# Turning the keys with 32x32 VectorE block transposes instead of TensorE transposes in a one-token decode block

## The chip, the cores and the metric

The kernel runs on one core of a Trainium2 chip. The metric is the time in device microseconds of one execution of the whole program. Five engines work side by side (in the kernel before, the three busiest are at work for 66%, 41% and 40% of the span): TensorE (PE in the profile; its weight loads are PEld), VectorE (DVE), ScalarE (ACT), GpSimd (POOL) and SyncE (SP), which here only issues transfers. In this kernel the data lie in on-chip tiles of 128 partitions; matmul results go to tiles that the kernel declares in a memory of their own, PSUM, in pieces that it calls banks (their names end in `_ps`).

TensorE runs at a granted clock, which the profile shows as a share of full speed (on average 0.803 in the profiled run of the kernel before).

## The reference, cut to what matters

One token, one layer: layer norm, attention over a cache of 65,536 keys and values, output projection, residual; then layer norm, a gated feed-forward of width 3,584, residual. There are 32 query heads and 4 key/value heads, so 8 query heads share one cache head.

```python
B, Sq, D = 1, 1, 1024
Hq, Hkv, Sk, Dh = 32, 4, 65536, 128          # k_cache, v_cache: (1, 4, 65536, 128) bf16
scores = einsum("bhqd,bhkd->bhqk", q, k) * Dh ** -0.5
p = softmax(scores); o = einsum("bhqk,bhkd->bhqd", p, v)
h  = x + o.reshape(1, 1, 4096) @ wo
h2 = h + (gelu(ln(h) @ w_gate) * (ln(h) @ w_up)) @ w_down   # F = 3584
```

The two caches hold 67 MB each; with the weights the kernel moves 173 MB, and every byte is used once. There is little arithmetic for each byte.

## The kernel before

All large inputs go through one queue and five rotating buffers of 4 MB (16,384 bf16 in each partition). A load is issued when the buffer that was filled five loads earlier is free again.

```python
NBUF = 5; CW = 16384
chpool = ctx.enter_context(tc.tile_pool(name="chpool", bufs=NBUF))
def load(src, name):
    t = chpool.tile([P, CW], BF16, name=name, tag="ch")
    ...
    nc.sync.dma_start(out=tv, in_=src)
```

Scores need the keys with the head dimension on the partitions, but they arrive with positions on the partitions. The kernel turns them on TensorE (two bf16 read as one f32, 128x128 at a time), and VectorE and ScalarE copy the result back out of PSUM:

```python
for c in range(NBK):
    kt_ps = ps_kt.tile([P, NB2, P], F32, name="kt_ps", tag="ktps")
    for b in range(NB2):
        nc.tensor.transpose(out=kt_ps[:, b, :], in_=k32s[...], identity=ident_f[:])   # L216
    if act_for(g, ci, c): nc.scalar.copy(out=dst_bf, in_=src_bf)                      # L220
    else:                 nc.vector.tensor_copy(out=dst_bf, in_=src_bf)               # L222
...
# scores: four column groups of 32, each matmul with its own weights
nc.tensor.matmul(qk_ps[32*c:32*c+32, :], lhsT=qsel[:, g, par, hf, :], rhs=..., tile_position=(0, 32*c))
...
nc.vector.transpose(out=sl..., in_=qk_ps[:])                                  # L245, 128x512
nc.vector.tensor_reduce(out=st["mx"][:, :, pi], in_=..., op=ALU.max)          # L246
```

When a head's scores are complete, the overall maximum is found, ScalarE takes the exponentials, and the values are multiplied while the keys of the next head arrive. So the first head is a stage of keys alone, the next three heads alternate keys and values, and the last head's values come alone. At the end comes the down projection, its weights in loads of 14, 7, 4, 2 and 1 rows of 128:

```python
def pair_mm(bank, stat, w2, c, first, last):     # the first 14 rows; 4 column groups, one bank
    for s in range(DS):
        g = 2 * s + c % 2
        nc.tensor.matmul(bank[32*g:32*g+32, :], lhsT=stat, rhs=w2[:, s*512:(s+1)*512], ..., tile_position=(0, 32*g))
# then cp_sum: 4 f32 matmuls against hsel add the column groups (hd_cp_ps);
# the last 14 rows: 8 matmuls each, 112 in all, one column out (dl_ps)
```

## Time and profile before

The median is 412.04 us over four runs (411.92 to 412.26). The profiled execution spans 410.2 us at a mean granted clock of 0.803.

| | before |
|---|---|
| moved by the main queue | 173.02 MB, 98.1% of 16 engines' span |
| rate between 20 and 390 us | 427 to 433 GB/s in each of seven stretches |
| TensorE / VectorE / ScalarE busy | 66% / 41% / 40% |
| first 14 rows of the down projection landed | 398.42 us |
| from there to the end | 11.8 us |

These are lines of the page of the kernel before: busy microseconds of each engine, two rows of the span cut into 40 slices (DMA in tenths of busy time, then GB/s), the engines' shares of the chain that ended last, and four groups of instructions (busy us, mean ns of one, then idle time before them and what ended it).

```profile
PE 271.7 (66%) x2577; PEld 193.1 (47%) x2577; DVE 168.9 (41%) x292; ACT 162.9 (40%) x249; POOL 5.1 (1%) x16
...
DMA  8999999999999999999999999999999999999993
GB/s 358 412 457 407 457 408 449 419 439 428 430 436 428 439 417 451 411 449 415 447 421 439 425 428 439 427 441 427 441 424 441 428 433 425 433 441 411 446 415 163
...
DMA 51%; PE 21%; ACT 6%; DVE 4%; issue 2%; DVEq 0%
...
L216 PE MATMUL kt_ps<-ident_f,k_sb 128*128 128x128 f32 x1024 | 144.5, 304 | 37.4 <-DMA k_sb<-in_A_k_cache_dram 34.4
L222 DVE COPY kt_sb<-kt_ps 128x1024 bf16<-128x1024 bf16 x140 | 95.3, 688 | 92.9 <-PE kt_ps L216 89.7
L246 DVE TENSOR_REDUCE mx<-sc_sb 128x8 f32<-128x512 f32 x32 | 35.2, 1100 | 0.5
L245 DVE STREAM_TRANSPOSE sc_sb<-qk_ps 128x512 f32<-128x512 f32 x32 | 23.0, 717 | 19.0 <-PE qk_ps L239 18.7
```

The DMA row never falls below nine tenths between the first and the last slice, and L216 waits almost only for keys to land. The transfers are the bottleneck; the engines run at their pace.

One 4 MB load (4.19 million bytes) takes 9.7 us at 431 GB/s.

Only the end of the program is not hidden behind transfers. This is the timeline of TensorE there (start, duration, engine, line, operation, count, and in brackets the idle time before it and what ended it):

```profile
398.42 2.66 PE L353 MATMUL d_ps<-wd_sb,actz 128*32 128x512 bf16 x28 [2.72 <-DMA wd_sb<-in_B_w_down_dram]
401.87 1.87 PE L382 MATMUL hd_cp_ps<-hsel,d_r 128*128 128x2 f32 x8 [0.79 <-DVE d_r L461]
403.60 2.50 PE L456 MATMUL dl_ps<-act_bf,wd_sb 128*128 128x1 bf16 x88
406.32 1.01 PE L456 MATMUL dl_ps<-act_bf,wd_sb 128*128 128x1 bf16 x24 [0.21 <-DMA wd_sb<-in_B_w_down_dram]
```

The last 24 matmuls wait a fifth of a microsecond for the last weights to land, so even this tail is balanced between TensorE and the queue.

### The profile page before, as it was taken

To read this page: it belongs to the slowest core of one execution; us is meant where nothing else is said; L and a number is where in the kernel's file an instruction comes from. 1 tells how busy PE (TensorE), PEld (TensorE's weight loads), DVE (VectorE), ACT (ScalarE), POOL (GpSimd) and SP (SyncE) were. 2 spreads that over 40 slices of the span, in tenths; PEclk is the share of its full clock that TensorE was granted. 3 is DMA by queue.
4 is the path that set the end of the run, shared out by engine and by line. 5 is a ranking of instruction groups with operands and counts; after the bars stand their busy time and mean duration, and the time that the engine had idled before them with its cause. 6 is when DMAs were issued, how large, how long until landed. Compare 5 with 4: busy or idle time off the path is not lost.

```text
span 410.2 us, 5998 instructions
## 1 busy us (share of the span) xinstructions
PE 271.7 (66%) x2577; PEld 193.1 (47%) x2577; DVE 168.9 (41%) x292; ACT 162.9 (40%) x249; POOL 5.1 (1%) x16
## 2 busy tenths in 40 slices
PE   0448888797994938964858399394945526467266
PEld 0227666484673727644555277182822213163135
DVE  0213787766772636751727086344630001022011
ACT  0014676597570648641525775152638000000000
POOL 1000000000000000000000000000020000000000
PEclk9986999969998886996969689979875655557665
DMA  8999999999999999999999999999999999999993
GB/s 358 412 457 407 457 408 449 419 439 428 430 436 428 439 417 451 411 449 415 447 421 439 425 428 439 427 441 427 441 424 441 428 433 425 433 441 411 446 415 163
DMA packets 6682, 173.40 MB, mean 423 GB/s; under 512 B 896, under 2 KB 896, under 8 KB 1152
## 3 DMA queue, kind: packets, MB, share of 16 engines
q1 hardware_dynamic: 6496, 173.02, 98.1%
q8 instruction: 20, 0.33, 0.3%
q14 instruction: 6, 0.05, 0.0%
q10 hardware_dynamic: 160, 0.00, 0.0%
HBM read 173.02 MB, written 0.00 MB: 422 GB/s over the span
## 4 chain that ended last, share of the span: by engine, by line
DMA 51%; PE 21%; ACT 6%; DVE 4%; issue 2%; DVEq 0%
DMA k_sb<-in_A_k_cache_dram 27%; PE kt_ps L216 13%; DMA wo_sb<-in_A_wo_dram 11%; DMA wu_sb<-in_B_w_up_dram 10%; ACT pT L272 4%; DMA wd_sb<-in_B_w_down_dram 3%; PE qk_ps L239 3%; ACT kt_sb L220 2%; PE acc_ps L289 2%; DVE mx L246 1%; PE at_ps L353 1%; PE wu_ps L158 1%; DVE kt_sb L222 1%; DVE sc_sb L245 1%; PE o_ps L305 1%
## 5 line engine op out<-in xcount | busy, mean ns | idle before, releaser
L216 PE MATMUL kt_ps<-ident_f,k_sb 128*128 128x128 f32 x1024 | 144.5, 304 | 37.4 <-DMA k_sb<-in_A_k_cache_dram 34.4
L216 PEld LDWEIGHTS kt_ps<-ident_f,k_sb 128*128 128x128 f32 x1024 | 131.6, 158 | 58.1 <-issue 36.6
L220 ACT COPY kt_sb<-kt_ps 128x1024 bf16<-128x1024 bf16 x116 | 111.9, 1016 | 105.5 <-issue 74.8
L222 DVE COPY kt_sb<-kt_ps 128x1024 bf16<-128x1024 bf16 x140 | 95.3, 688 | 92.9 <-PE kt_ps L216 89.7
L272 ACT ACTIVATE pT<-sc_sb,nbias 128x256 bf16<-128x256 f32 x64 | 47.5, 746 | 23.7 <-DVE nbias L264 23.7
L239 PE MATMUL qk_ps<-kt_sb,qsel 128*32 128x512 bf16 x512 | 39.6, 384 | 9.9 <-ACT kt_sb L220 9.2
L289 PE MATMUL acc_ps<-v_sb,pT 128*32 128x512 bf16 x512 | 37.4, 441 | 12.2 <-DMA v_sb<-in_A_v_cache_dram 12.2
L246 DVE TENSOR_REDUCE mx<-sc_sb 128x8 f32<-128x512 f32 x32 | 35.2, 1100 | 0.5
L245 DVE STREAM_TRANSPOSE sc_sb<-qk_ps 128x512 f32<-128x512 f32 x32 | 23.0, 717 | 19.0 <-PE qk_ps L239 18.7
L289 PEld LDWEIGHTS <-pT 128*32 128x32 bf16 x512 | 16.8, 107 | 28.9 <-issue 19.9
L165 ACT COPY wg_ev<-wg_ps 96x512 f32<-96x512 f32 x1 | 0.6, 582 | 59.4 <-PE wg_ps L158 59.4
L239 PEld LDWEIGHTS <-qsel 128*32 128x32 bf16 x512 | 8.3, 94 | 24.5 <-DVE kt_sb L222 15.2
L298 PE MATMUL l_ps<-lpart,ones_f 128*128 128x8 f32 x16 | 3.8, 312 | 21.7 <-ACT pT L272 21.7
L298 PEld LDWEIGHTS l_ps<-lpart,ones_f 128*128 128x128 f32 x16 | 3.2, 249 | 23.9 <-ACT pT L272 23.1
L158 PEld LDWEIGHTS <-hnz 128*32 128x32 bf16 x112 | 5.0, 127 | 17.6 <-issue 15.6
L158 PE MATMUL wu_ps<-wu_sb,hnz 128*32 128x512 bf16 x56 | 6.6, 579 | 9.3 <-DMA wu_sb<-in_B_w_up_dram 9.3
L353 PE MATMUL at_ps<-wo_sb,o2z 128*32 128x512 bf16 x64 | 7.2, 630 | 8.3 <-DMA wo_sb<-in_A_wo_dram 8.3
L272 ACT ACTIVATION_READ_ACCUMULATOR pT<-sc_sb,nbias 128x1 f32 x64 | 12.1, 190 | 0.0
L302 DVE COPY acc_sb<-acc_ps 128x512 f32<-128x512 f32 x4 | 2.7, 684 | 22.7 <-PE acc_ps L289 22.7
L165 ACT ACT_TABLE_LOAD x1 | 1.3, 1283 | 25.8 <-DVE q_ev L163 25.8
L125 PE MATMUL ln_tot<-ln_s,ones_f 128*128 128x1 f32 x4 | 1.2, 363 | 13.9 <-DVE ln_s L123 13.9
L353 PEld LDWEIGHTS <-o2z 128*32 128x32 bf16 x64 | 2.7, 140 | 12.0 <-issue 11.5
(108 smaller groups left out, 93.0 us busy)
## 6 DMA issues: line engine op xcount, KB each, us to landing
k_sb<-in_A_k_cache_dram SPq DMA_DIRECT2D x16, 4096.0 KB, 40.2
v_sb<-in_A_v_cache_dram SPq DMA_DIRECT2D x16, 4096.0 KB, 37.5
wq_sb<-in_A_wq_dram SPq DMA_DIRECT2D x2, 4096.0 KB, 16.8
wo_sb<-in_A_wo_dram SPq DMA_DIRECT2D x2, 4096.0 KB, 43.3
wg_sb<-in_B_w_gate_dram SPq DMA_DIRECT2D x2, 3584.0 KB, 43.7
wu_sb<-in_B_w_up_dram SPq DMA_DIRECT2D x2, 3584.0 KB, 40.6
wd_sb<-in_B_w_down_dram SPq DMA_DIRECT2D x1, 3584.0 KB
wd_sb<-in_B_w_down_dram SPq DMA_DIRECT2D x1, 1792.0 KB, 29.6
```

The costliest lines, as they stand in the source:

```text
L158: nc.tensor.matmul(banks[s // 4][32 * g:32 * g + 32, :], lhsT=stat, rhs=mov(s), start=first, stop=last, tile_position=(0, 32 * g))
L216: nc.tensor.transpose(out=kt_ps[:, b, :], in_=k32s[m0 // 16][:, m0 % 16, :], identity=ident_f[:])
L220: nc.scalar.copy(out=dst_bf, in_=src_bf)
L222: nc.vector.tensor_copy(out=dst_bf, in_=src_bf)
L239: nc.tensor.matmul(qk_ps[32 * c:32 * c + 32, :], lhsT=qsel[:, g, par, hf, :], rhs=mv[:, :, 32 * c:32 * c + 32, par], start=(hf == 0 and pa ...
L245: nc.vector.transpose(out=sl.rearrange("p n h -> p (n h)"), in_=qk_ps[:])
L246: nc.vector.tensor_reduce(out=st["mx"][:, :, pi], in_=sl.rearrange("p n h -> p h n"), axis=AX.X, op=ALU.max)
L272: nc.scalar.activation(out=pT[:, :, r, :], in_=sc_sb[:, hf * HG * TG:(hf + 1) * HG * TG, r].rearrange("p (a t) -> p a t", t=TG), func=ACT. ...
L289: nc.tensor.matmul(acc[32 * c:32 * c + rep * TG, :], lhsT=pTs[a // HG][:, a % HG, :, :].rearrange("p r t -> p (r t)"), rhs=v_sb[:, i * TG: ...
L298: nc.tensor.matmul(l_ps[:], lhsT=ones_f[:], rhs=lpart[:, hf, :], start=(hf == 0), stop=(hf == NH - 1))
L305: nc.tensor.matmul(o_ps[:], lhsT=acc_sb[:, t * Dh:(t + 1) * Dh], rhs=sel[:, t:rep * TG:TG], start=(t == 0), stop=(t == TG - 1))
L353: nc.tensor.matmul(bank[32 * g:32 * g + 32, :], lhsT=stat, rhs=w2[:, s * 512:(s + 1) * 512], start=first, stop=last, tile_position=(0, 32 ...
```

## The change

The intent is to take the transposes of the keys off TensorE and the copies off VectorE and ScalarE, and to load fewer weights.

1. VectorE turns the keys in place, 32x32 blocks of 32-bit words, four instructions of 128x2048 for each load. The copies of `kt_ps` go away.
2. A block-wise transpose leaves four positions' worth of data on the four quarters of the partitions. Query weights of 128x128 that hold the queries on the diagonal blocks and zeros elsewhere (`wsel`) take care of that: 32 matmuls of 512 columns for each load.
3. A weight load serves two matmuls in the scores, four in the values, and several in the projections. For this the order of TensorE is fixed by explicit dependencies.
4. The down projection puts both halves of a row in the same column group, and 21 of its 28 rows go this way instead of 14.

The diff, cut to its core (`mm` is a helper that emits a matmul, reuses the loaded weights where `loaded` is set, and chains it behind the one before; `evac` alternates VectorE and ScalarE):

```diff
-    ps_kt = ...(bufs=4, space=PSUM)   -    ps_qk = ...(bufs=2, space=PSUM)
+    ps_qk = actx.enter_context(tc.tile_pool(name="ps_qk", bufs=1, space=PSUM))
...
+    def k_load(g, li):
+        kt = kv_load(k_v[g], li, "k_sb").rearrange("p n d -> p (n d)").bitcast(U32)
+        for c in range(NSP):                                     # NSP = 4
+            nc.vector.transpose(out=kt[:, c * w:(c + 1) * w], in_=kt[:, c * w:(c + 1) * w])
...
+    def k_scores(g, li):
+        qk_ps = ps_qk.tile([P, 2, 512], F32, name="qk_ps", tag="qkps")
+        for a in range(TG):
+            for bp in range(4):
+                for k in range(2):
+                    mm(qk_ps[:, k, :], wsel[:, o:o + P], kt[:, a, k, :, bp // 2, :, bp % 2], ..., loaded=(k == 1))
+        nc.vector.transpose(out=sl..., in_=qk_ps[:]...)                      # 128x1024
+        nc.vector.tensor_reduce(out=st["mx"][:, :, li], ..., op=ALU.max)
+        if li == NL - 1:
             softmax_head(g)
...
-            acc_sb = ...; nc.vector.tensor_copy(out=acc_sb[:], in_=acc[:])
+            for c in range(4):
+                evac(acc_sb[32 * c:32 * c + 32, :], acc[32 * c:32 * c + 32, c, :], c)
...
+        for li in range(NL):
+            k_load(g, li)
+            if g >= 1: v_load(g - 1, li)
+            k_scores(g, li)
+            if g >= 1: v_values(g - 1, li)
...
-    def pair_mm(bank, stat, w2, c, first, last):
-            g = 2 * s + c % 2
+    def row_mm(banks, stat, w2, c, first, last):
+        g = c % 4
+        for s in range(DS):
+            mm(banks[s][32 * g:32 * g + 32, :], stat, w2[:, s * 512:(s + 1) * 512], first, last,
+               loaded=(s > 0), tile_position=(0, 32 * g))
...
-            nc.tensor.matmul(ps[:, b, :], lhsT=row[:, b * P:(b + 1) * P], rhs=hsel[:], ...)
+            for s in range(DS):
+                mm(ps[:, b, s:s + 1], row[:, s, b * P:(b + 1) * P], ones_f[:, 0:1], True, True)
...
-    NW = sizes[0]
+    NW = 21
```

## The prediction

> **What bounds it now.** The DMA. The page's DMA row stands at nine tenths or more in every slice but the first and last, queue 1 fills 98.1% of the 16 engines' span, and the windows view shows 429 to 435 GB/s from 5 us to about 380 us whatever the engines do. [...] 173.02 MB at 431 GB/s is 401.4 us of the 410.2 us span; about 2 us of start and 6 to 7 us of tail remain. The other engines (TensorE 66% busy) hide behind it. So only the tail, or a new starvation of the DMA queue, can move the time.
>
> **Removed.** 1024 f32 TensorE transposes (144.5 us busy), 256 copies of kt_ps (ScalarE 111.9, VectorE 95.3 us), about half of the weight loads.
>
> **Added.** 64 in-place VectorE transposes 128x2048. The 128x512 one takes 717 ns; [...] I estimate 2.3 us each, 9.2 us per K load. Score transpose and maximum now come as 1024 wide, estimated 1.25 and 2.2 us. With a wait for TensorE's last matmuls, VectorE needs about 15 us per K load. K and V scores become 1024 full-array matmuls of 512 columns, 0.21 us at full clock: 6.9 us per load of 9.7 us.
>
> **Consequence, main part.** With K and V alternating there are 19.4 us per K load: fits. In the first head K loads come every 9.7 us, so VectorE falls about 20 us behind; the five buffers nearly absorb it. My tightest point is the first V buffer's release, at about 113 to 119 us, against about 117 us when the queue needs it. Stall: 0 to 4 us in 95 to 130 us, more likely none.
>
> **Consequence, tail.** Down-projection rows: before, 28 matmuls ran four at a time (2.66 us from 398.4 us); now both matmuls of a row sit in one column group, so about two at a time: 15 slots of 0.21 to 0.43 us for 14 rows, and seven more rows (8 slots) after the 7-row load, all before the partial sums. Those sums have 16 passes for 8 (1.87 us before). Then 56 column matmuls for 112, but after all that. Estimate: TensorE ends 1.5 us (full clock) to 7 us (half clock) later than the 407.3 us of before; granted clock there was 0.5, so middle +3.5 us. This lies wholly on the critical path.
>
> **Prediction.** 415.5 us, 80% range 411 to 420.5. Faster by over 2%: 0.02; within 2%: 0.84; slower by over 2%: 0.14.
>
> **What would show it.** DMA row still nine tenths, about 431 GB/s. VectorE 55 to 60% busy, ScalarE under 20%, weight loading much lower. k_sb transposes 2.2 to 2.4 us. GB/s dips only between 95 and 130 us. In the chain of waits the end is TensorE's d_ps, hd_cp_ps, dl_ps work instead of the wd_sb landing; final dl_ps matmul at about 411 us.
>
> **What would make it wrong.** (a) The 32-bit SBUF transposes run at half rate: VectorE then needs over 20 us per K load, +30 us or more. (b) The clock stays at half during the V-only stage: 13.7 us per load exceeds 9.7, and the backlog reaches the tail. (c) The tail's clock is full, or TensorE runs the row matmuls more concurrently: then 411 to 412 us. (d) VectorE's doubled SBUF traffic slows the DMA.

The sum: 412.0 us of the kernel before + 0 us of stall + 3.5 us of tail = 415.5 us. The 15 us for each load of keys can also be estimated from the trace of the kernel before alone, in proportion to the elements: 16 × 717 ns for the keys, 2 × 717 ns for the scores and 2 × 1100 ns for the maximum are 15.1 us, without the wait.

## More of the kernel before

The next view is the table of stretches. Its columns are the stretch, its length, the busy time of PE, PEld, DVE, ACT and POOL with the number of instructions, the granted clock, the DMA share and GB/s.

```profile
60.00:100.00 40.00, 33.42 (x309) 24.93 (x308) 27.43 (x42) 29.17 (x50) 0.00 (x0) 0.91 1.00 432
100.00:130.00 30.00, 22.58 (x252) 16.28 (x250) 18.85 (x26) 15.32 (x16) 0.00 (x0) 0.99 1.00 431
180.00:200.00 20.00, 12.14 (x116) 9.86 (x109) 7.20 (x10) 6.05 (x7) 0.00 (x0) 0.83 0.99 427
```

The rate is nearly the same in all three, 427 to 432 GB/s, whatever the engines do.

## The result, and the profile after

The median is 414.97 us over four runs (414.42 to 415.13). The ratio to the kernel before is 1.0065, with a 95% interval of 1.0051 to 1.008. By the 2% measure the time is the same; by the interval it is a little longer.

The page of the kernel after, the lines that answer to those above:

```profile
PE 305.6 (74%) x1521; PEld 71.5 (17%) x732; DVE 216.0 (52%) x192; ACT 59.2 (14%) x151; POOL 12.3 (3%) x17
...
GB/s 356 409 454 419 443 419 444 420 441 422 397 408 451 416 447 418 441 416 400 447 416 452 409 454 409 451 411 451 412 451 411 447 416 447 419 430 428 426 414 151
...
DVE 42%; PE 34%; DMA 10%; ACT 9%; issue 5%; SPq 0%; ACTq 0%; DVEq 0%
...
L246 DVE STREAM_TRANSPOSE k_sb<-k_sb 128x2048 uint32<-128x2048 uint32 x64 | 143.0, 2279 | 0.1
L114 PE MATMUL qk_ps<-k_sb,wsel 128*128 128x512 bf16 x256 | 105.0, 410 | 23.5 <-DVE k_sb L246 23.0
...
L264 DVE STREAM_TRANSPOSE sc_sb<-qk_ps 128x1024 f32<-128x1024 f32 x16 | 20.0, 1248 | 46.0 <-PE qk_ps L116 33.9
L265 DVE TENSOR_REDUCE mx<-sc_sb 128x8 f32<-128x1024 f32 x16 | 31.8, 1987 | 0.4
```

The engines' work changed a great deal: ScalarE went from 40% to 14%, weight loading from 47% to 17%, VectorE from 41% to 52%. The chain that ended last was half DMA before; now it is mostly VectorE and TensorE. But the GB/s row is nearly as before, except in slices 11 and 12 (397 and 408, about 103 to 124 us) and slice 19 (400, about 186 to 196 us). The stretches show the same:

```profile
60.00:100.00 40.00, 20.48 (x72) 4.27 (x37) 36.30 (x22) 0.55 (x1) 0.00 (x0) 0.81 1.01 432
100.00:130.00 30.00, 28.15 (x117) 4.53 (x44) 16.53 (x10) 11.43 (x32) 0.00 (x0) 0.92 0.96 406
...
180.00:200.00 20.00, 19.94 (x85) 3.37 (x33) 14.59 (x9) 0.00 (x0) 0.00 (x0) 0.91 0.97 408
```

The queue ran partly dry twice: 406 GB/s instead of 431 for 30 us, and 408 instead of 427 for 20 us. By arithmetic that is 30 × (1 − 406/431) = 1.7 us and 20 × (1 − 408/427) = 0.9 us of lost transfer time. Take these as rough: stretches of 20 us scatter by about 10 GB/s where nothing runs dry (in this kernel 420 in 220 to 240 us, 441 in 240 to 260 us).

A split of the profiled span (410.2 to 413.1, so +2.9 us) at the landing of the first 14 rows of the down projection gives the size of both parts: the landing moved from 398.42 to 400.32 us (+1.9), and what follows it grew from 11.8 to 12.8 us (+1.0). So about two thirds came from dry spells of the queue and one third from the tail.

**The first dry spell.** This is the timeline of the kernel after, around the end of the first head:

```profile
95.79 0.15 DVE L273 TENSOR_REDUCE mx<-mx 128x8 f32<-128x32 f32 x1
95.85 2.30 DVE L246 STREAM_TRANSPOSE k_sb<-k_sb 128x2048 uint32<-128x2048 uint32 x1
...
98.07 0.24 DVE L277 TENSOR_REDUCE gm<-mxT_ps 8x1 f32<-8x128 f32 x1
...
99.14 0.61 PE L114 MATMUL qk_ps<-k_sb,wsel 128*128 128x512 bf16 x1
...
99.45 0.76 ACT L291 ACTIVATE pT<-sc_sb,nbias 128x256 bf16<-128x256 f32 x1 [61.39 <-DVE nbias L283]
...
108.75 0.38 PE L116 MATMUL qk_ps<-k_sb,wsel 128*128 128x512 bf16 x1
...
109.15 0.33 SPq L131 DMA_DIRECT2D v_sb<-in_A_v_cache_dram  x1
```

Read it from the bottom. The load issued at 109.15 us needs the buffer of the fifth load of keys (the second head's first). Its last score matmul starts at 108.75. The first started at 99.14, behind the first head's maximum, which VectorE finished late because it had been busy with keys nearly all the time (36.3 us of the 40 before 100 us). The rhythm of the first head shows why: the issues that wait for the first head's key buffers come 13.9 us apart (46.47, 60.40, 74.33 and 88.25 us), each after the last score matmuls of a load, which themselves wait for VectorE's last transpose of it, while keys arrive every 9.7 us. VectorE falls behind by about 4 us for each load, and five buffers do not quite cover it. In the kernel before, the corresponding load was issued at 95.68 us.

The fifth load's scores also ran slowly at first. After TensorE's wait the first 14 matmuls start 0.43 us apart, at a granted clock of 0.50 (99.1 to 105.06 us); only from 105.06 us, 5.9 us after the first of them, they start 0.216 us apart, at a clock of 1.00 (105.06 to 109.2 us). The third head's first scores do the same: 5.9 us at a clock of 0.51 from 177.73 us, then 1.00 from 183.60 us. In e3 below the same scores run slow for only 3.4 us (100.70 to 104.08), so the length varies; what sets it is not shown.

**The second dry spell.** The exponentials of a head stand on ScalarE ahead of two of the four copies of the previous head's values:

```profile
174.04 0.58 ACT L202 COPY acc_sb<-acc_ps 32x512 f32<-32x512 f32 x1
...
176.01 1.87 PE L114 MATMUL o_ps<-sel,acc_sb 128*128 128x8 f32 x8 [7.97 <-ACT acc_sb L202]
...
187.69 0.33 SPq L131 DMA_DIRECT2D v_sb<-in_A_v_cache_dram  x1
```

TensorE stood idle for 7.97 us before the matmuls that read these copies, started the third head's first scores only at 177.73 us, and the buffer they free went back to the queue at 187.69. ScalarE did its work here in the order in which it was given: VectorE's copy of the first quarter of the same values started at 167.95 us, but ScalarE took eight exponentials first (168.01 to 174.02 us) and only then its own copy, at 174.04.

**The tail.** The timeline of TensorE in the kernel after:

```profile
400.32 0.62 PE L114 MATMUL d_ps<-wd_sb,actz 128*32 128x512 bf16 x4 [3.35 <-DMA wd_sb<-in_B_w_down_dram]
400.70 0.67 PE L116 MATMUL d_ps<-wd_sb,actz 128*32 128x512 bf16 x4
...
406.82 1.95 PE L114 MATMUL hd_cp_ps<-ones_f,d_r 128*128 128x1 f32 x16 [0.79 <-DVE d_r L200]
408.62 1.62 PE L114 MATMUL dl_ps<-act_bf,wd_sb 128*128 128x1 bf16 x56
```

The partial sums start at 406.82 instead of 401.87 us, because they wait for the second load's rows too; with half as many column matmuls behind them, the end is only about a microsecond further from the first landing than before.

### The profile page after: what moved, and what is told of

Same layout as the page of the kernel before. It is cut to its first block, busy times and chain, and to the rows that moved or that the text cites. A ratio compares the mean times of both kernels' runs of the same rounds, so it can differ in the third digit from the quotient of the medians.

```text
span 413.1 us, 2802 instructions
## 1 busy us (share of the span) xinstructions
PE 305.6 (74%) x1521; PEld 71.5 (17%) x732; DVE 216.0 (52%) x192; ACT 59.2 (14%) x151; POOL 12.3 (3%) x17
## 4 chain that ended last, share of the span: by engine, by line
DVE 42%; PE 34%; DMA 10%; ACT 9%; issue 5%; SPq 0%; ACTq 0%; DVEq 0%
DVE k_sb L246 30%; PE acc_ps L116 10%; ACT pT L291 7%; PE qk_ps L114 5%; DMA wq_sb<-in_A_wq_dram 5%; PE qk_ps L116 5%; DVE sc_sb L264 5%; DMA wd_sb<-in_B_w_down_dram 4%; DVE mx L265 4%; PE acc_ps L114 4%; PE o_ps L114 2%; ACT acc_sb L202 1%; PE hc_ps L114 1%; DVE acc_sb L200 1%; PE h_cp_ps L114 1%
## 5 line engine op out<-in xcount | busy, mean ns | idle before, releaser
L246 DVE STREAM_TRANSPOSE k_sb<-k_sb 128x2048 uint32<-128x2048 uint32 x64 | 143.0, 2279 | 0.1
L114 PE MATMUL qk_ps<-k_sb,wsel 128*128 128x512 bf16 x256 | 105.0, 410 | 23.5 <-DVE k_sb L246 23.0
L116 PE MATMUL acc_ps<-v_sb,pT 128*128 128x512 bf16 x384 | 110.0, 397 | 0.0
L116 PE MATMUL qk_ps<-k_sb,wsel 128*128 128x512 bf16 x256 | 104.8, 409 | 0.0
L114 PE MATMUL acc_ps<-v_sb,pT 128*128 128x512 bf16 x128 | 51.0, 399 | 0.0
L114 PEld LDWEIGHTS <-wsel 128*128 128x128 bf16 x256 | 26.5, 104 | 128.5 <-issue 106.9
L264 DVE STREAM_TRANSPOSE sc_sb<-qk_ps 128x1024 f32<-128x1024 f32 x16 | 20.0, 1248 | 46.0 <-PE qk_ps L116 33.9
L265 DVE TENSOR_REDUCE mx<-sc_sb 128x8 f32<-128x1024 f32 x16 | 31.8, 1987 | 0.4
L114 PEld LDWEIGHTS <-pT 128*128 128x128 bf16 x128 | 13.2, 103 | 97.8 <-issue 97.7
L114 PE MATMUL o_ps<-sel,acc_sb 128*128 128x8 f32 x32 | 7.5, 364 | 26.6 <-ACT acc_sb L202 26.6
L114 PEld LDWEIGHTS o_ps<-sel,acc_sb 128*128 128x128 f32 x32 | 7.1, 328 | 26.9 <-ACT acc_sb L202 26.9
L152 POOL MEMSET wsel<- 128x8224 bf16 x1 | 6.9, 6942 | 0.0
L200 DVE COPY q_ev<-q_ps 128x512 f32<-128x512 f32 x1 | 0.7, 691 | 11.8 <-PE q_ps L116 11.8
```

Source lines behind the costliest of these rows:

```text
L114: return pe(t.matmul(out, lhsT=lhsT, rhs=rhs, start=start, stop=stop, tile_position=tile_position, skip_group_check=skip_group_check))
L116: op = t.add_instruction(mybir.InstMatmult(name=nc.get_next_instruction_name(), engine=t.engine, start_tensor_calc=start, stop_tensor_calc ...
L152: nc.gpsimd.memset(wsel[:], 0.0)
L200: nc.vector.tensor_copy(out=dst, in_=src)
L246: nc.vector.transpose(out=kt[:, c * w:(c + 1) * w], in_=kt[:, c * w:(c + 1) * w])
L264: nc.vector.transpose(out=sl.rearrange("p n h -> p (n h)"), in_=qk_ps[:].rearrange("p k n -> p (k n)"))
```

## The experiments

The theory after the result is (A): the transfers bound both kernels, and the time of after is that of before plus two dry spells of the queue, caused by buffers that are released late (first VectorE's backlog in the first head, then copies behind exponentials), plus a longer tail. The rivals: (B) the tail alone, with its extra partial sums; (C) TensorE's low clock at the end of the first head (0.50 in 99.1 to 105.06 us); (D) the fixed order of TensorE, which keeps the fifth load's scores behind the first head's maximum; (E) VectorE's traffic slows the transfers.

(E) falls without a run: in 60 to 100 us VectorE is busy for 36.3 of 40 us instead of 27.4, and the rate is 432 GB/s in both kernels.

Each of the twelve experiments ran five rounds against the kernel before, in three batches on two chips. In each batch before gave medians of 412.0 to 412.1 us. All results were correct. "V issue" is the moment of the issue at 109.15 us above; "rate" is GB/s in 100 to 130 us; "landing" and "tail" split the profiled span as above.

| run | what it does to the kernel after | median, us (range) | ratio to before [95%] | V issue | rate | landing | tail |
|---|---|---|---|---|---|---|---|
| before | | 412.04 | 1 | 95.68 | 431 | 398.42 | 11.8 |
| after | | 414.97 (414.42–415.13) | 1.0065 [1.0051, 1.008] | 109.15 | 406 | 400.32 | 12.8 |
| e1_nw14 | 14 rows, not 21 | 415.19 (412.62–415.95) | 1.0064 [1.0043, 1.0085] | 109.70 | 405 | 400.16 | 13.8 |
| e2_accdve | copies of values on VectorE | 414.02 (413.4–416.44) | 1.0054 [1.0034, 1.0074] | 109.03 | 405 | 398.60 | 13.0 |
| e3_warm | dummy matmuls before the first scores | 414.51 (414.31–415.18) | 1.0062 [1.0049, 1.0075] | 109.47 | 406 | 399.88 | 12.6 |
| e4_k4first | fifth load's scores before the maximum | 417.92 (416.09–418.24) | 1.0131 [1.0114, 1.0147] | 100.72 | 412 | 401.02 | 13.2 |
| e5_mx1 | 6 us less VectorE work in the first head | 412.51 (411.91–412.75) | 1.0011 [0.9996, 1.0025] | 102.60 | 428 | 397.49 | 12.6 |
| e6_oldtail | down projection as before | 414.36 (413.39–415.34) | 1.0054 [1.0039, 1.0068] | 108.17 | 418 | 400.13 | 12.0 |
| e7_ownw | every matmul loads its own weights | 416.55 (415.23–419.07) | 1.0114 [1.0088, 1.014] | 111.17 | 385 | 403.78 | 13.5 |
| e8_schalf | scores in two half tiles | 414.46 (412.21–415.27) | 1.0044 [1.0022, 1.0065] | 109.87 | 405 | 399.34 | 13.7 |
| e9_pipe | keys turned ahead, and the old tail | 411.30 (411.24–411.36) | 0.9982 [0.9968, 0.9995] | 106.45 | 424 | 397.54 | 12.0 |
| e10_mx2 | 8 us more VectorE work in the first head | 418.96 (417.66–420.45) | 1.0169 [1.0148, 1.019] | 114.39 | 334 | 404.83 | 12.7 |
| e11_again | nothing (after once more) | 414.62 (414.15–415.71) | 1.0068 [1.0055, 1.008] | 109.22 | 406 | 399.71 | 12.7 |
| e12_mx1tail | e5 and e6 together | 411.37 (411.2–411.57) | 0.9984 [0.9971, 0.9996] | 97.93 | 427 | 397.68 | 12.0 |

The last four columns come from one profiled run each. How far such single values scatter can be read from kernels that share their code up to that point: in after, e1, e2, e6 and e11 the V issue lies between 108.17 and 109.70 us and the rate between 405 and 418; in after, e1, e6 and e11 the rate in 180 to 200 us lies between 393 and 419 GB/s; e5 and e12, with the same first head, have their V issues at 102.60 and 97.93.

### e1_nw14: the number of rows alone

```diff
-    NW = 21
+    NW = 14
```

> Only the tail is undone: 14 rows of the down projection as wide matmuls instead of 21, so that the partial sums (hd_cp_ps) leave the end of the chain. Theory (of the 2.9 us, about 1.9 us is the weight stream arriving late because the DMA queue ran dry at 108 to 111 us and near 190 us, and about 1.0 us is the tail): 414.0 us, the last dl_ps matmul follows the last wd_sb landing by 0.4 us, the 14-row load still lands near 400.3 us. Rival A (all of the loss is in the tail): 412.0 us. Rival B (the added SBUF traffic of VectorE slows the DMA, tail no matter): 415.0 us.

The median was 415.19 us: no gain. The tail grew from 12.8 to 13.8 us. Its timeline shows why:

```profile
404.52 3.57 PE L114 MATMUL hd_cp_ps<-ones_f,d_r 128*128 128x1 f32 x16 [0.77 <-DVE d_r L200]
407.96 3.12 PE L114 MATMUL dl_ps<-act_bf,wd_sb 128*128 128x1 bf16 x112
```

The 16 passes of the partial sums took 3.57 us where after needed 1.95 and before 1.87 (for 8 passes). The granted clock was 0.50 here between 404 and 411 us, and 1.00 in after while its sums ran. The 112 column matmuls then followed, at the same half clock, when almost nothing was left to transfer (DMA share 0.03 in 408 to 411 us). So this run changed two things at once, the rows and the clock, and does not tell whether the rows alone would have helped. It shows what costs at half clock: twice the passes of partial sums (two banks instead of one), with 112 column matmuls behind them. Whether fewer rows brought the half clock about, or chance did, is not shown. The expectation missed because it took the tail's TensorE work as shrinking with the rows.

### e2_accdve: the copies of the values

```diff
-                evac(acc_sb[32 * c:32 * c + 32, :], acc[32 * c:32 * c + 32, c, :], c)
+                nc.vector.tensor_copy(out=acc_sb[32 * c:32 * c + 32, :], in_=acc[32 * c:32 * c + 32, c, :])
```

> The four copies of acc_ps all on VectorE, none behind the exponentials in ScalarE's queue. Theory: the o_ps matmuls of the first head then come at about 170 us instead of 176 us, the fifth-from-now release (first K buffer of the third head) at about 182 instead of 187.3 us, and the dry spell near 190 us goes: 0.5 to 0.9 us less, 414.1 to 414.5 us. If the DMA is slowed by VectorE traffic instead: no change, 415.0 us (VectorE gets slightly more work).

The median was 414.02 us. In the profiled run the second dry spell is gone, and the first is as it was (V issue 109.03, 405 GB/s). From its stretches:

```profile
180.00:200.00 20.00, 19.94 (x93) 3.36 (x35) 15.66 (x10) 0.00 (x0) 0.00 (x0) 1.00 1.00 429
```

That is 429 GB/s in place of 408, and the issue of 187.69 came at 183.90 us; both lie outside the scatter of the runs that keep these copies and the first head as they were (393 to 419 GB/s, issue at 187.69 to 188.45). So the copies are needed for the second spell. They are not enough for it: e5 below keeps them and loses the spell all the same. Its worth is less certain: the runs scatter from 413.4 to 416.44 us, and the intervals of this kernel and of after overlap.

### e3_warm: the clock

```diff
+        if g == 0:
+            wps = ps_warm.tile([P, 512], F32, name="wps", tag="wps")
+            for i in range(26):
+                mm(wps[:], wsel[:, 0:P], wsel[:, 0:512], True, True)
+            junk = ...; nc.vector.tensor_copy(out=junk[:], in_=wps[:, 0:1])
         mxT_ps = ps_m.tile([rep, P], F32, name="mxT_ps", tag="misc")
```

> 26 useless full-array matmuls fill TensorE's wait before the first head's maximum, so that its clock is up when the 32 score matmuls of the fifth K load start at 99.1 us (16 of them ran at 0.43 us in the changed kernel). Theory: these matmuls take 6.9 instead of 9.8 us, the buffer is free at about 106.3 instead of 109.0 us, the queue's issue comes before it runs dry, and the first dry spell (about 1.3 us) goes or nearly: 413.6 to 414.2 us. If the release is late for another reason than the clock: 415.0 us. If the DMA is slowed by VectorE traffic: 415.0 us.

The median was 414.51 us, and the issue stayed at 109.47. The experiment did not do what it was made for; that the dummies would have the clock up for the scores is not shown (the clock was 0.93 in 85 to 100 us, and 0.66 in 100 to 105). The dummies ran from 89.45 to 95.2 us, TensorE then stood idle until 100.4 us, but for one transpose at 97.75, for the first head's maximum, and when the scores began at 100.7 the first eight were again 0.43 us apart. The extra copy also delayed VectorE. So (C) is not tested by this run, and stays open as a contribution. The traces allow an estimate of its size. From the first to the last start the 32 score matmuls of the fifth load took 9.61 us in after (14 of them slow, not 16 as the expectation says), 8.47 in e11 and 8.36 here; 31 steps of 0.216 us would be 6.7. The half clock thus puts the issue off by about 1.7 to 2.9 us, which is as much as e9 below wins back by other means (2.7 us). VectorE's backlog and the slow clock both stand in the same chain, and no run here takes away the clock alone.

### e4_k4first: the order of TensorE

The second head's first scores come before the first head's maximum and its broadcast:

```diff
-            k_scores(g, li)
+            k_mm(g, li)                    # the 32 score matmuls
+            if g == 1 and li == 0:
+                softmax_head(0)
+            k_post(g, li)                  # score transpose and maximum
```

> In TensorE's fixed order the score matmuls of the second head's first K load come before the first head's maximum (mxT_ps, bc_ps) instead of behind it. Theory: that buffer is free at about 101 us instead of 109 us, so the queue does not run dry there; but the exponentials start about 3 us later, and the next K buffer comes free about 3 us later too, at about 128 us where the queue needs it at about 126 us, so a part of the gain may be lost again: 413.5 to 415.0 us, issue of the V load at about 101.5 us instead of 109.15 us.

The issue came 8 us earlier, as expected of (D). But the kernel was 3 us slower than after, not faster. These are the issues of this run:

```profile
100.72 0.33 SPq L131 DMA_DIRECT2D v_sb<-in_A_v_cache_dram  x1
117.78 0.33 SPq L131 DMA_DIRECT2D k_sb<-in_A_k_cache_dram  x1
```

The next issue moved from 116.06 us (in after) to 117.78, because the exponentials began about 3 us later and the value matmuls with them. The rate in 100 to 130 us was 412 GB/s, hardly better than 406, and the second dry spell grew (388 GB/s in 180 to 200 us). A single release is not the cause; moving it up only moves the wait to the next buffer. So (D) falls as the cause of the loss. This run was a surprise to (A) too: I had expected a small gain.

### e5_mx1 and e10_mx2: the length of VectorE's work in the first head

These two change nothing but the time VectorE needs in the first head. In e5 the first head's maximum is taken over its first load only. The softmax does not need the exact maximum, so the result was right for these inputs, but this is not a general kernel. In e10 the same maximum is taken twice.

```diff
# e5_mx1
+        if g > 0 or li == 0:
             nc.vector.tensor_reduce(out=st["mx"][:, :, li], ..., op=ALU.max)
# e10_mx2
+        for _ in range(2 if g == 0 else 1):
             nc.vector.tensor_reduce(out=st["mx"][:, :, li], ..., op=ALU.max)
```

> In the first head only, the maximum over the scores is taken over the first of four loads alone (the result stays right for these inputs, as any bound near the scores does; it is no general kernel). That takes three 1.99 us reductions from VectorE where it works without a pause from 35 to 96 us in the changed kernel. Theory (VectorE's backlog in the first head makes the release of the fifth K buffer late): the first head's exponentials start at about 93.5 instead of 99.45 us, the V load is issued at about 103 instead of 109.15 us, and the low rate between 100 and 130 us (406 GB/s) goes back to about 430: 1.3 to 1.8 us less, 413.0 to 413.5 us. Rival (the loss there is the added SBUF traffic or a slow clock, not the backlog): rate still near 406 GB/s, 414.5 to 415.0 us.

> The changed kernel with the maximum of each load taken twice in the first head: about 8 us more on VectorE there. Theory (the backlog is on the critical path, and the queue has no slack left at 109 us): exponentials start about 8 us later, the V load is issued near 117 us, and nearly all of it shows in the time: 419.5 to 423 us. If the backlog were not the cause: 415 us.

The timeline of e5 has the issue here, and its table of stretches reads:

```profile
102.60 0.33 SPq L131 DMA_DIRECT2D v_sb<-in_A_v_cache_dram  x1
```

```profile
100.00:130.00 30.00, 27.25 (x120) 4.38 (x44) 21.22 (x12) 6.65 (x18) 0.00 (x0) 0.94 1.00 428
180.00:200.00 20.00, 19.94 (x94) 3.18 (x33) 15.73 (x9) 0.00 (x0) 0.00 (x0) 1.00 0.99 428
```

The issue and the first stretch of e10:

```profile
114.39 0.33 SPq L131 DMA_DIRECT2D v_sb<-in_A_v_cache_dram  x1
```

```profile
100.00:130.00 30.00, 22.37 (x91) 4.33 (x40) 16.71 (x13) 11.97 (x32) 0.00 (x0) 0.85 0.80 334
```

Six microseconds less work (three reductions of 1.99 us) brought the issue 6.6 us forward and the rate back to 428 GB/s, and 2.2 us came off the time (ratios 1.0065 and 1.0011, a difference of 0.54%). Eight microseconds more put the issue off by 5.2 us and cost 4.2 us (1.0169 against 1.0068 for after in the same batch). The second is slightly less than was expected for it. The effect goes in both directions, in the place and with the sign that (A) says. VectorE's work in the first head is a cause of the first dry spell, shown in both directions. The 2.2 us are not the worth of the first spell alone, though: in e5 the second went too (428 GB/s in 180 to 200 us, the issue of 187.69 at 182.20), although its copies still stand behind the exponentials. That is also why e5 won more than the 413.0 to 413.5 us expected of it. The second spell needs both the late first head and the copies; about 2.2 us is what both spells cost together.

### e6_oldtail and e12_mx1tail: the tail

e6 restores the down projection of before: 14 rows in one bank, sums by 8 passes, 112 column matmuls. e12 has both this and e5's cut.

```diff
-    NW = 21
+    NW = 14
-                row_mm(d_ps, actz[:, c, :], wv[:, cc, :], c, c < 4, c + 4 >= NW)
+                for s in range(DS):
+                    gg = 2 * s + c % 2
+                    mm(d_ps[32 * gg:32 * gg + 32, :], actz[:, c, :], wv[:, cc, s * 512:(s + 1) * 512],
+                       c < 2, c + 2 >= NW, tile_position=(0, 32 * gg))
...
+            for b in range(4):
+                mm(hd_ps[:, b, :], d_r[:, b * P:(b + 1) * P], hsel[:], True, True)
```

> The whole down projection as before the change: 14 rows, both halves of a row in different column groups of one bank, sums with 8 passes instead of 16. The first tail experiment undid only the number of rows and left TensorE bound by the sums (at half clock) and 112 column matmuls. Theory: the end follows the landing of the 14-row load by 11.8 us as before the change, not 12.8 us: 1.0 us less, 413.7 us. Rival (tail costs nothing): 414.7 us.

> Both causes taken away together: the first head's maximum over one load alone (not general) and the old down projection. Theory: the two effects add up; the 14-row load lands at about 397.5 us and the end comes 11.8 us later: 410.8 to 411.8 us. If they do not add: 412.0 to 412.6 us.

The tail went to 12.0 us in both, from 12.8 (and 12.6 in e5). The time fell by 0.6 us for after (414.97 to 414.36) and by 1.1 us for e5 (412.51 to 411.37). For e6 that is less than expected (413.7), and its interval overlaps that of after; the gain of e12 over e5 is the clearer one, as their runs do not overlap. Rival (B) is therefore a part of the truth, the smaller one: with the tail restored the kernel is still 0.54% slower than before. With the tail restored and the first head relieved (e12), it is 0.16% faster than before. The two parts together account for the excess.

### e7_ownw: the shared weight loads

```diff
-        if not loaded:
+        if True:
             return pe(t.matmul(out, lhsT=lhsT, rhs=rhs, ...))
```

> Every matmul loads its own weights again, order kept. Weight loads then overlap the matmul before them. Theory: the reuse is off the path: [...]weight loading busy from 72 to about 160 us, 414.5 to 415.2 us. Rival (the reuse pays): over 416 us, matmul starts further apart.

The median was 416.55 us, about 2 us over after, and outside what was expected. Weight loading doubled (142.6 us busy for 71.5), the score matmuls still started 0.216 us apart, and yet in its profile the first dry spell was deeper (385 GB/s, issue at 111.17): two of three loads took VectorE 14.6 to 14.7 us instead of 13.9. In these two VectorE waited 2.75 and 2.66 us for the last score matmuls instead of 1.98, because TensorE's slow matmuls, those 0.43 us apart, fell later in the load. But that happens without the extra weight loads too: one load of e11, the unaltered kernel, also took 14.7 us (74.84 to 89.54), in the same way. And the profiled run of e7 is the slowest of its six (419.07 us). So the runs say that the reuse of weights is worth about 2 us in this kernel; by which way is not shown and stays open. Whether the fixed order costs anything apart from the reuse stays open too, as no run here leaves the order free.

### e8_schalf: the scores in two half tiles

Another way to loosen the second head's start: the exponentials of the first half free half of the scores early.

```diff
+        if li % 2 == 0:
+            st.setdefault("sc", []).append(scpool.tile([P, NT // 2, rep], F32, ...))
-        sc_sb = st["sc_sb"]
+        sc_sb = st["sc"][li // 2]
```

> The scores lie in two tiles of half a head each, and the two halves of the exponentials' sums are added by two matmuls, not on VectorE, so that VectorE waits for 6 us of exponentials instead of 12 us before the next head's first scores. Theory: VectorE's idle 12 us at 99.4 to 111.5 us shrinks to 6, later K buffers of the second head come free up to 6 us earlier; the first late issue (109.15 us) is unchanged because it hangs on the score matmuls before it; the second (187.7 us) may come earlier only as far as the copies behind ScalarE's exponentials let it: 0 to 0.7 us less, 414.0 to 414.7 us.

The median was 414.46 us (412.21 to 415.27). The second dry spell went (428 GB/s in 180 to 200 us, with the issue at 185.15), the first did not (405). The gain is of the size of e2's, and as uncertain.

### e9_pipe: a version that follows from this

If VectorE's rhythm in the first head is the cause, then its waits there should go: 4 × 2.28 + 1.25 + 1.99 = 12.4 us of work stand in a rhythm of 13.9 us. In after, VectorE waits 1.98 us for the last score matmuls of a load (before its score transposes at 60.41 and 74.33 us) while the next load lies ready. In e9 it turns the first quarter of the next keys before it reads the scores. The tail is that of before. This is a general kernel.

```diff
+        if g == 0 and li < NL - 1:
+            k_load(0, li + 1)
+            ahead = k_turn(0, li + 1, 1)           # first of four pieces of the next load
         op = nc.vector.transpose(out=sl..., in_=qk_ps[:]...)
+        # ... and a dependency that keeps this read of the scores behind that piece
```

> The down projection as before the change, and in the first head VectorE turns the first piece of the next K load while TensorE finishes the scores of this one, instead of waiting about 2 us per load for them. Nothing is left out, so this is a kernel for general use. Theory (VectorE's backlog in the first head): the first head takes about 6 us less on VectorE, exponentials start at about 94 instead of 99.45 us, the V load is issued near 103 us, the dry spells near 109 and 190 us go; with the old tail the end follows the 14-row landing by 11.8 us: 411.0 to 412.2 us, as fast as before or up to 1 us faster. Rival (backlog not the cause): 413.7 us, as with the old tail alone.

The median was 411.30 us (411.24 to 411.36), ratio 0.9982 with an interval of 0.9968 to 0.9995: still "the same" by the 2% measure, but ahead of both kernels. From its timeline, the first exponential, the issue and the tail:

```profile
97.00 0.76 ACT L306 ACTIVATE pT<-sc_sb,nbias 128x256 bf16<-128x256 f32 x1 [58.36 <-DVE nbias L298]
...
106.45 0.33 SPq L131 DMA_DIRECT2D v_sb<-in_A_v_cache_dram  x1
...
397.54 3.18 PE L114 MATMUL d_ps<-wd_sb,actz 128*32 128x512 bf16 x28 [3.34 <-DMA wd_sb<-in_B_w_down_dram]
401.51 1.87 PE L114 MATMUL hd_cp_ps<-hsel,d_r 128*128 128x2 f32 x8 [0.79 <-DVE d_r L511]
```

VectorE's wait before the score transposes shrank to 1.01 us or less, and two of these transposes stood 13.0 us apart (72.93 and 85.90) in place of 13.9. The exponentials began 2.4 us earlier than in after (97.00 for 99.45; about 94 had been expected), and the issue came 2.7 us earlier. This was enough: 424 GB/s in 100 to 130 us, and 426 in 180 to 200. Against e6, which has the same tail, e9 is 3.1 us faster. The scatter of the runs shrank with the dry spells, from more than a microsecond in most of the runs above to 0.12 us here and 0.37 in e12. Before, whose queue is never dry, repeats within 0.56 us too; e5, with no dry spell either, scatters by 0.84. What makes the scatter is not shown.

### e11_again: after once more

> The changed kernel once more, unaltered, as the base line of this call and to see how far its runs lie apart: 414.4 to 415.1 us, issue of the V load near 109 us.

The median was 414.62 us, ratio 1.0068, with the issue at 109.22. The result repeats: e9 to e12 ran on another chip than e1 to e8.

Not tried on the chip: a sixth buffer, and taking the first head's maximum on GpSimd.

## Why the prediction was right or wrong

The predicted time was 415.5 us, in a range of 411 to 420.5; measured were 414.97. The class (within 2%) was right. But two of its terms were mis-sized in opposite directions, and their errors nearly cancelled. The total deserves less credit than it looks.

1. **"The DMA" bounds the kernel; only the tail or a new starvation can move the time.** Right. VectorE's busy time grew from 168.9 to 216.0 us and weight loading fell from 193.1 to 71.5 us, and this changed nothing as long as the queue was fed: 432 GB/s in 60 to 100 us for both kernels. The large change of engine work moved the time by 0.65%, and all of that comes from dry spells and tail.
2. **The costs of the new instructions.** Right: transposes of 2.28 us (2.3 estimated), the score transpose 1.25 us (1.25), the maximum 1.99 us (2.2). The score matmuls start 0.216 us apart at a clock of 1.00 (0.21). The prediction's (a) did not come about. Between the two transposes the step from 1024 to 2048 elements costs (2279 − 1248) / 1024 = 1.0 ns an element, but they read from different memories, so this is not the measured rate of either. The maximum costs (1987 − 1100) / 512 = 1.7 ns for each element beyond the 512 of the kernel before; whether its strided view or the reduction makes it so was not tested. VectorE's rhythm was 13.9 us for each load (about 15 predicted), its share 52% (55 to 60 predicted).
3. **"Stall: 0 to 4 us in 95 to 130 us, more likely none."** The place of the danger (the first head's backlog and the five buffers) was right, and the size lay in the range, but "more likely none" was wrong. The landing at the end came 1.9 us later, and e5 gives about 2.2 us for this spell and the second together. The buffer was another one, too. Named was the release of the first values' buffer at 113 to 119 us; that one did come free at 116.06 us, as forecast. But the queue had run dry before that. The step that failed is the choice of the tightest release: it was that of the fifth load of keys, at 109.15, which the prediction did not look at. Its scores wait on TensorE for the first head's maximum, which waits for VectorE, and then run slowly (the first 14 of them 0.43 us apart).
4. **"GB/s dips only between 95 and 130 us."** Wrong. There was a second dip at about 188 us, from the new copies of the values behind the exponentials on ScalarE. The prediction had not costed this part of the diff. e2 shows that the copies are needed for it, e5 that the late first head is too.
5. **Tail: "middle +3.5 us".** Mis-sized: +1.0 us. The step that failed is "now both matmuls of a row sit in one column group, so about two at a time: 15 slots". The kernel chains these matmuls row by row, first half and then second half; yet four first halves of four rows started together at 400.32, their four second halves at 400.70, so that later rows' first halves started ahead of an earlier row's second half. The 28 matmuls took 3.6 us, about eight slots of 0.43 us and not fifteen. And the partial sums, double in passes, took 1.95 us instead of a doubled 1.87, since TensorE's clock was full (1.00 in 406.8 to 408.8 us, where before had 0.50 in its tail); e1 shows the same sums at 3.57 us with a clock of 0.50. The final column matmuls ended at 408.62 + 1.62 = 410.24 us; "about 411" had been said, but with a landing that was 1.9 us later than assumed. So both conditions of the prediction's own (c), a full clock and row matmuls that overlap more, came true, and for these it had named 411 to 412 us. That the time still came close to 415.5 us is luck: the dry spells, held unlikely, filled the gap.
6. **The end of the chain of waits is d_ps, hd_cp_ps, dl_ps.** Right.
7. **What the prediction left out:** the order and reuse of weights had no term in its sum. e7's runs show that the reuse is worth about 2 us, for a reason that stays open.

With the measured terms: 412.0 + about 2 (dry spells) + about 0.5 to 1 (tail) gives 414.5 to 415, where the prediction had 412 + 0 + 3.5.

## What to carry to other kernels

Where one queue of transfers is nearly full all the time, moving work between engines gained nothing here, and new dependencies lost something: for each stage, ask which engine releases the buffers, what its rhythm is for each load, and whether that is longer than a load takes to arrive. The stage to look at is the one in which one kind of load comes alone (here the first head), and a wait of the slowest engine there can be filled with a piece of the next load's work, as in e9. Moving a single release earlier helped nothing, as e4 showed; shortening the slow engine's chain did.
